# Padding the weight and activation loads to 128 and 112 partitions, with four norm rows and a free instruction order in the key loop

## Chip, cores and metric

The kernel runs on one core of one Trainium2 chip. The metric is the device time of one launch in microseconds (us), lower is better. Every time below is a median of several runs. The engines are PE (matmul; PEld is its weight load), DVE (vector), ACT (scalar), POOL, and SP, which issues most loads and stores here.

## The reference

One transformer block with adaptive layer norm, 2048 tokens, width 576, 32 heads of 18, feed-forward width 4608, all in bf16. Cut to what matters:

```python
mod = (silu(c) @ w_mod).reshape(1, 6, 1, -1)          # shift/scale/gate, twice
sa, ca, ga, sb, cb, gb = (mod[:, i] for i in range(6))
h = layernorm(x) * (1 + ca) + sa
x = x + ga * attention(h)     # q, k, v = h @ wqkv; linear attention: phi = softmax(+-(q or k) @ w_phi)
                              # kv = phi_k^T v ; o = (phi_q kv) / (phi_q sum(phi_k)) ; o @ wo
h = layernorm(x) * (1 + cb) + sb
x = x + gb * (relu(h @ w1) @ w2)
```

## The kernel before

The first layer norm is never applied to x. Instead x, turned (features on partitions, loaded from memory as `xT`), is multiplied by weights that carry the scale, and the mean and the shift come in as extra rows: two unused feature rows, 96 and 97 of the last feature chunk, hold the mean and the standard deviation of each token ("norm rows"), and the weights get matching rows. The 576 features plus padding are cut into NC = 5 chunks of R = 116 partitions. So `xT`, the weights and the modulation weights are all tiles of 116 partitions, and the head groups of the fold (`wq` or `wk` times `w_phi`) are tiles of GR = 108.

```python
R = 116
F = NC * R
X0 = 96
NX = X0 + 2                       # two norm rows, partitions 96 and 97
GR = 108
...
    ctx.enter_context(tc.manual_schedule())        # every engine follows the source order
...
    def load_xT(b):
        t0, nt = BLK[b]
        o = XOFF[t0][0]
        sp.dma_start(xT[0:R, o:o + NC * nt * P], a["xT"][:, o:o + NC * nt * P])

    load(act, ccol[0:R, :], "cc")
    load(act, flat(bdw[0:GR]), "bdw")
    load_x(0, 2)                                   # x itself: 128 partitions, for the statistics
    load(sp, flat(wsc[0:R]), "wsc")                # scale modulation weights
    load(act, ident[:], "ident")
    load(sp, flat(wkT[0:GR]), "wkT")               # key weights, turned
    load_xT(0)
    load(sp, flat(wsh[0:R]), "wsh")                # shift modulation weights
    load_x(2, 2)
    load(sp, flat(wv_raw[0:R]), "wv")
    load_xT(1)
    load_x(4, 2)
    ...                                            # wqT, xT(2), wcb, wsb
    load_x(6, 4)
    load_x(10, 6)
    ...
```

The start computes the scale modulation (`mods([wsc])`), folds the key weights (`fold_k`, five chunks: PE, then ACT, then DVE on one bank pair), the shift modulation, the norm rows of the weights (`rows_mm`, `rows_e`), and the keys of tiles 0 and 1. Then the key loop:

```python
    for t in range(2, NT):
        proj(S0, t - 2, wv)              # values of tile t-2: "the first value projection" is t = 2
        k_sums(t - 1)
        v_e(t - 2, S0)
        k_r(t - 1)
        if t % 2 and t + 1 < NT:
            x_rows(t + 1)                # stat_mm(t+1, 4): statistics transposed into PSUM bank 4
        ...
        proj(S1, t, wk)                  # keys of tile t
        exps(t, S1, E_sb[:, t % NE, :])
        ...
        if t <= 6:
            fold_mm(wqT, t - 2, S2)      # bank pair 4, 5
            fold_e(S2, wq, t - 2, act)
        ...
        if t + 4 < NT:
            bn(0, t + 4)                 # DVE: statistics of tile t+4, needs x of that tile
            if t % 2:
                stats(t + 3)
```

After it come the last queries and the output projection (the tail), then the feed-forward: two matmul loops, `l1` and `l2`, over eight pairs of tiles.

The softmax here doesn't subtract the row's maximum and nothing guards it: scores larger than these inputs give would overflow.

## Time and profile before

| | before |
|---|---|
| time, median of 4 runs (467.32 to 468.48) | 468.12 us |
| span of the profiled run | 466.6 us |
| scale weights' first matmul | 12.9 us |
| first value projection | 40.5 us |
| x tiles 6 to 9 landed | 64 us |
| first feed-forward matmul | 151.4 us |
| feed-forward to the end | 315.1 us |

The first fence holds three lines of the page's overview of before, the span in 40 slices of 11.7 us: the granted PE clock in tenths, the mean busy share of the DMA engines in tenths, and the rate in GB/s.

```profile
PEclk9559559998999999999999999999999999999999
DMA  5346343247370652022123113102211210110000
GB/s 156 114 142 162 114 155 109 98 153 306 75 257 0 243 66 43 14 55 39 41 41 41 43 25 70 41 14 55 41 28 43 50 42 15 30 36 20 0 1 27
```

In the first six slices, 70 us, the clock falls to a half and the loads reach only 114 to 162 GB/s, while the tenth slice shows that 306 is to be had. The next fence is the chain of work that ended last, of before, in its first 66 us: start, duration, and what the time went to.

```profile
2.32 23.87 DMA R<-in_wsh_dram
26.21 5.26 SPq L163
31.52 3.48 SPq L163
35.04 29.12 DMA x_sb<-in_xk_dram
64.19 0.83 DVE st L207 x2
```

The chain is two transfers and the issue of transfers (`SPq`): the shift weights, then the x tiles 6 to 9. Nothing computed is on it until 64.19 us. The waits of before in 0 to 70 us (waiter, releaser, us in total, how often, the longest):

```profile
DVE st L207 <- DMA x_sb<-in_xk_dram: 20.6, 2, 18.5
ACT rk L293 <- DVE Rk L276: 20.2, 2, 18.6
PE PS L237 <- ACT R L511: 16.8, 1, 16.8
PEld L230 <- DMA R<-in_wsc_dram: 6.1, 1, 6.1
```

DVE waited 18.5 us for x; ACT (18.6) waited for DVE's sum behind it, and PE (16.8, the fold of the query weights, L237) for ACT. One wait, seen three times. Last, sums by stretch of before: start and end, length, busy time of PE, PEld, DVE, ACT and POOL, then granted clock, DMA share and GB/s.

```profile
28.00:40.00 12.00, 8.20 (x55) 6.72 (x55) 6.00 (x18) 4.00 (x11) 0.40 (x1) 0.61 0.25 101
50.00:56.00 6.00, 0.68 (x3) 0.36 (x2) 0.00 (x0) 0.00 (x0) 0.00 (x0) 0.50 0.25 106
101.00:112.00 11.00, 9.28 (x69) 6.74 (x68) 6.00 (x12) 6.75 (x13) 5.86 (x8) 0.84 0.90 387
151.60:466.60 315.00, 311.04 (x2873) 254.75 (x2870) 155.70 (x307) 51.59 (x103) 17.03 (x24) 1.00 0.20 43
```

With 116-partition loads in flight the share is 0.25 and the rate 101 to 106 GB/s; with a 128-partition load it is 0.90 and 387. Counted from the packet times of the trace, 4 packets were under way at once for 93% of 50 to 56 us, and 16 for 93% of 101 to 112 us. The feed-forward keeps PE busy for 311 of 315 us and is untouched by the change.

### The profile page before, as it was taken

How to read it: one execution, taken by the hardware profiler on the slowest of the kernel's cores; microseconds unless marked ns; L12 is line 12 of the kernel's file. 1: busy time of each engine (PE TensorE's matmuls, PEld its weight loads, DVE VectorE, ACT ScalarE, POOL GpSimd, SP SyncE). 2: the span in 40 equal slices, each digit the busy share in tenths (PEclk: the TensorE clock that was granted, in tenths of full speed). 3: DMA queues.
4: the chain of work that ended last, by engine and by line, in shares of the span. 5: the costliest groups of instructions: out<-in, count | busy, mean ns of one | idle time of the engine just before them, and what ended most of it. 6: DMA issues, size and time to landing. Idle time of an engine off the chain costs nothing.

```text
span 466.6 us, 8766 instructions
## 1 busy us (share of the span) xinstructions
PE 418.4 (90%) x3810; PEld 336.6 (72%) x3810; DVE 231.5 (50%) x448; ACT 128.8 (28%) x281; POOL 58.6 (13%) x97
## 2 busy tenths in 40 slices
PE   5748229889997999999999999999999999999996
PEld 1536117767875887888888788788888878878885
DVE  2244047755964454475366445537635653453321
ACT  1215128766856320121031013012103101300210
POOL 1002014344930010020011002002001100000000
PEclk9559559998999999999999999999999999999999
DMA  5346343247370652022123113102211210110000
GB/s 156 114 142 162 114 155 109 98 153 306 75 257 0 243 66 43 14 55 39 41 41 41 43 25 70 41 14 55 41 28 43 50 42 15 30 36 20 0 1 27
DMA packets 43752, 35.03 MB, mean 75 GB/s; under 512 B 38541, under 2 KB 40826, under 8 KB 43330
## 3 DMA queue, kind: packets, MB, share of 16 engines
q1 hardware_dynamic: 42754, 23.68, 20.8%
q10 hardware_dynamic: 960, 10.79, 5.9%
q8 instruction: 30, 0.49, 0.4%
q14 instruction: 8, 0.07, 0.0%
HBM read 22.80 MB, written 2.36 MB: 54 GB/s over the span
## 4 chain that ended last, share of the span: by engine, by line
PE 78%; DMA 11%; ACT 5%; SPq 2%; DVE 2%; issue 1%; ACTq 0%
PE PS L663 30%; PE PS L621 28%; PE PS L266 9%; DMA x_sb<-in_xk_dram 6%; DMA R<-in_wsh_dram 5%; PE PS L407 4%; PE PS L628 4%; SPq L163 2%; ACT EQ L271 2%; PE PS L382 1%; ACT E_sb L271 1%; PE PS L325 1%; PE PS L360 1%; DVE Rk L276 1%; ACT RH L244 0%
## 5 line engine op out<-in xcount | busy, mean ns | idle before, releaser
L663 PE MATMUL PS<-R,RH 128*128 128x288 bf16 x1152 | 144.7, 286 | 0.0
L621 PE MATMUL PS<-h,R 128*128 128x256 bf16 x1152 | 134.4, 274 | 0.0
L663 PEld LDWEIGHTS <-RH 128*128 128x128 bf16 x1152 | 112.7, 98 | 28.2
L621 PEld LDWEIGHTS <-R 128*128 128x128 bf16 x1152 | 110.4, 98 | 18.0 <-issue 5.1
L636 ACT ACTIVATE RH<-PS 128x512 bf16<-128x512 f32 x72 | 43.0, 598 | 183.4 <-PE PS L628 162.3
L638 DVE TENSOR_SCALAR RH<-PS 128x512 bf16<-128x512 f32 x72 | 49.8, 692 | 67.9 <-PE PS L628 36.4
L266 PE MATMUL PS<-RH,R 116*128 116x288 bf16 x480 | 70.8, 302 | 5.7 <-ACT EQ L271 3.6
L266 PEld LDWEIGHTS <-R 116*128 116x128 bf16 x480 | 47.8, 103 | 19.8 <-issue 6.9
L666 DVE TENSOR_TENSOR yt<-PS,gb_row 128x288 f32<-128x288 f32 x32 | 14.7, 458 | 63.8 <-PE PS L663 62.7
L207 DVE BATCH_NORM_STATS2 st<-x_sb 128x6 f32<-128x288 bf16 x60 | 24.3, 446 | 21.1 <-DMA x_sb<-in_xk_dram 20.6
L339 POOL TENSOR_TENSOR ratq<-Rq,rq 128x32 f32<-128x32 f32 x16 | 4.1, 254 | 216.5 <-DVE rq L336 216.1
L276 DVE TENSOR_REDUCE Rk<-E_sb 128x64 f32<-128x1152 bf16 x16 | 21.4, 1335 | 14.4 <-ACT E_sb L271 14.4
L271 ACT ACTIVATE E_sb<-PS,rs 128x576 bf16<-128x576 f32 x32 | 22.0, 738 | 6.0 <-PE PS L266 5.8
L271 ACT ACTIVATE EQ<-PS,rs 128x576 bf16<-128x576 f32 x32 | 21.9, 743 | 4.3 <-PE PS L266 4.3
L407 PE MATMUL PS<-wo_sb,oT 128*128 128x288 bf16 x160 | 22.5, 286 | 0.0
L237 PE MATMUL PS<-bdw,R 108*116 108x108 bf16 (+1 forms) x60 | 6.2, 262 | 17.8 <-ACT R L511 16.8
L276 DVE TENSOR_REDUCE Rq<-EQ 128x64 f32<-128x1152 bf16 x16 | 21.5, 1341 | 0.0
L411 ACT ACTIVATE lnv<-mv,eps_t 128x1 f32<-128x1 f32 x16 | 4.7, 296 | 58.8 <-DVE mv L208 57.9
L237 PEld LDWEIGHTS <-R 108*116 108x116 bf16 (+1 forms) x60 | 6.2, 185 | 18.9 <-issue 18.6
L628 PE MATMUL PS<-h,R 64*128 64x256 bf16 x288 | 19.9, 271 | 0.0
L283 POOL TENSOR_TENSOR E_sb<-E_sb,rat 128x576 bf16<-128x576 bf16 x16 | 18.6, 1166 | 1.3
L283 POOL TENSOR_TENSOR EQ<-EQ,ratq 128x576 bf16<-128x576 bf16 x16 | 18.6, 1165 | 1.3
(87 smaller groups left out, 281.1 us busy)
## 6 DMA issues: line engine op xcount, KB each, us to landing
R<-in_w1a_dram ACTq DMA_DIRECT2D x1, 4608.0 KB
R<-in_w2a_dram ACTq DMA_DIRECT2D x1, 2592.0 KB
R<-in_w2b_dram ACTq DMA_DIRECT2D x1, 2592.0 KB
out_dram<-x_sb SPq DMA_DIRECT2D x16, 144.0 KB
R<-in_xT_dram SPq DMA_DIRECT2D x3, 580.0 KB
x_sb<-in_xk_dram SPq DMA_DIRECT2D x3, 288.0 KB
x_sb<-in_xk_dram SPq DMA_DIRECT2D x1, 864.0 KB
R<-in_wkT_dram SPq DMA_DIRECT2D x1, 734.1 KB
```

What stands on the lines that cost most here:

```text
L207: dve.bn_stats(out=s[:, hf, :], in_=x_sb[:, t, hf * HD:(hf + 1) * HD])
L266: pe.matmul(pr[:, k, 0:HD], lhsT=xt(t, ck), rhs=w[0:R, ck, k * HD:(k + 1) * HD], start=(ck == 0), stop=(ck == NC - 1))
L271: act.activation(out=E.rearrange("p (b h s e) -> p b h s e", b=2, s=2, e=DH)[:, :, :, s, :], in_=pr[:, :, 0:HD].rearrange("p b (h e) -> p ...
L276: dve.tensor_reduce(out=Rr, in_=E.rearrange("p (c e) -> p c e", e=DH), axis=AXX, op=ALU.add)
L283: eng.tensor_tensor(out=e, in0=e, in1=ratio.unsqueeze(2).to_broadcast([P, H, DH]), op=ALU.mult)
L407: pe.matmul(pr[:, k, 0:HD], lhsT=oT[:, t % 2, ci, :], rhs=wo_sb[:, ci, k * HD:(k + 1) * HD], start=(ci == 0 and not add_x), stop=(ci == NC ...
L621: pe.matmul(PS[:, 2 * u + hf, n * 256:n * 256 + 256], lhsT=w1a[:, ci, jj * P:(jj + 1) * P], rhs=hb[:, ci, :], start=(n == 0 and ci == 0), ...
L628: pe.matmul(PS[:, 2 * u + hf, n * 256:n * 256 + 256], lhsT=w1b[b0:b0 + 64, j * P:(j + 1) * P], rhs=hb[b0:b0 + 64, 4, :], start=False, stop ...
L636: act.activation(out=o, in_=i, func=ACT.Relu)
L638: dve.tensor_relu(o, i)
L663: pe.matmul(PS[:, bank, 0:HD], lhsT=H1[:, j % 18, j // 18, tt * P:(tt + 1) * P], rhs=w2[j // 18][:, j % 18, k * HD:(k + 1) * HD], start=(j ...
L666: dve.tensor_tensor(out=yt[:, k, :], in0=PS[:, bank, 0:HD], in1=gb_row[:, c], op=ALU.mult)
```

## The change

The intent: send every large load as 128 (or 112) full partitions, to have it at a rate like the 387 GB/s of the 128-partition load in before instead of the 101 to 106 of the 116-partition ones; put the weights that the start needs first ahead of x; carry the mean as two bf16 parts, with a second pair of norm rows, for accuracy; and let the instruction scheduler order the key loop and the tail, where before the source order was kept on every engine. In the start only PE keeps the source order. The diff, cut to its core:

```diff
-NX = X0 + 2
+NX = X0 + 4
 GR = 108
+GP = 112
@@
-    ctx.enter_context(tc.manual_schedule())
+    PEO = {mybir.EngineType.PE}
@@ loads (all 116-row ones alike; the arrays in memory are padded with zero rows)
-        sp.dma_start(xT[0:R, o:o + NC * nt * P], a["xT"][:, o:o + NC * nt * P])
+        sp.dma_start(xT[:, o:o + NC * nt * P], a["xT"][:, o:o + NC * nt * P])
-    load(act, ccol[0:R, :], "cc")
-    load(act, flat(bdw[0:GR]), "bdw")
+    load(act, ccol[:], "cc")
+    load(act, flat(bdw[0:GP]), "bdw")
+    load(act, ident[:], "ident")
+    load(sp, flat(wsc), "wsc")
+    load(sp, flat(wkT[0:GP]), "wkT")
+    load_xT(0)
     load_x(0, 2)
-    load(sp, flat(wsc[0:R]), "wsc")
-    load(act, ident[:], "ident")
-    load(sp, flat(wkT[0:GR]), "wkT")
-    load_xT(0)
-    load(sp, flat(wsh[0:R]), "wsh")
+    load(sp, flat(wsh), "wsh")
+    load(sp, flat(wv_raw), "wv")
     load_x(2, 2)
-    load(sp, flat(wv_raw[0:R]), "wv")
... (the rest in the old order, padded)
@@ norm rows: mean as two parts
-        act.activation(out=sc[:, t % 4:t % 4 + n, X0], in_=mv[:, 0, t:t + n, 0], func=ACT.Copy)
+        act.activation(out=sc[:, t % 4:t % 4 + n, X0:X0 + 3:2], in_=mv[:, 0, t:t + n, 0:1].to_broadcast([P, n, 2]), func=ACT.Copy)
+        pool.tensor_tensor(out=sc[:, t % 4:t % 4 + n, X0 + 3], in0=mv[:, 0, t:t + n, 0], in1=sc[:, t % 4:t % 4 + n, X0], op=ALU.subtract)
@@ rows_e: one copy becomes two steps
+        act.activation(out=h, in_=i, func=ACT.Copy)
+        dve.scalar_tensor_tensor(out=o, in0=h, scalar=mk[X0:NX, :], in1=i, op0=ALU.mult, op1=ALU.add)
@@ order
-    spin(14, 0)
+    order = ExitStack()
+    order.enter_context(tc.manual_schedule(engines=PEO))
+    spin(11, 0)
... (the start rewritten: folds first, statistics of x after them)
+    kv_eps()
+    order.close()                       # from here on free, until the feed-forward
... (key loop and tail as they were)
+    ctx.enter_context(tc.manual_schedule())
     NB = NT // 2
```

More of the change, by code (lines that the diff above doesn't have):

```diff
@@ L87, in tile_block @@
     wo_sb = small([P, NC, D], BF16, "wo_sb")
-    ident = small([P, P], BF16, "ident")
+    ident = small([P, P + 1], BF16, "ident")
+    mk = small([P, 1], FP32, "mk")
     mask = small([P, KVW], BF16, "mask")
@@ L121, in tile_block @@
     yt = small([P, 2, HD], FP32, "yt")
+    tmpr = yt.rearrange("p a b -> p (a b)").bitcast(BF16)[:, 0:D]
     stg = yt.rearrange("p a b -> p (a b)").bitcast(BF16)[:, 0:4 * P]
@@ L180, in tile_block @@
     load(sp, epsr[:], "epsr")
-    load(sp, flat(wqT[0:GR]), "wqT")
+    load(sp, flat(wqT[0:GP]), "wqT")
     load_xT(2)
-    load(sp, flat(wcb[0:R]), "wcb")
-    load(sp, flat(wsb[0:R]), "wsb")
+    load(sp, flat(wcb), "wcb")
+    load(sp, flat(wsb), "wsb")
     load_x(6, 4)
@@ L187, in tile_block @@
     load_xT(3)
-    load(sp, flat(wga[0:R]), "wga")
+    load(sp, flat(wga), "wga")
     load(sp, flat(wo_sb), "wo")
-    load(sp, flat(wgb[0:R]), "wgb")
+    load(sp, flat(wgb), "wgb")
     load_xT(4)
@@ L195, in tile_block @@
     pool.memset(eps_t[:], EPS)
+    pool.tensor_copy(mk[:], ident[:, P:P + 1])
     pool.memset(m98[:], 0.0)
@@ L219, in stat_mm @@
         for j in range(n):
-            pe.transpose(bf(PS[:, bank, :])[0:NX, j * P:(j + 1) * P], sc[:, (t + j) % 4, :], ident[:])
+            pe.transpose(bf(PS[:, bank, :])[0:NX, j * P:(j + 1) * P], sc[:, (t + j) % 4, :], ident[:, 0:P])
         return bf(PS[:, bank, :])[X0:NX, 0:n * P]
@@ L254, in rows_mm, with rows_e @@
                           start=(ck == 0), stop=(ck == NC - 1))
-    def rows_e(pr, dst, eng):
-        o, i = v2(dst[X0:NX, 4, :]), pr[X0:NX, :, 0:HD]
-        if eng is act:
-            act.activation(out=o, in_=i, func=ACT.Copy)
-        else:
-            eng.tensor_copy(out=o, in_=i)
+    def rows_e(pr, dst):
+        o, i, h = v2(dst[X0:NX, 4, :]), pr[X0:NX, :, 0:HD], v2(tmpr[X0:NX, :])
+        act.activation(out=h, in_=i, func=ACT.Copy)
+        dve.scalar_tensor_tensor(out=o, in0=h, scalar=mk[X0:NX, :], in1=i, op0=ALU.mult, op1=ALU.add)
     def proj(pr, t, w, cks=range(NC)):
@@ L395, in o_turn_pe @@
         for ci in range(NC):
-            pe.transpose(pt[:, ci * P:(ci + 1) * P], o_sb[:, t % 2, ci * P:(ci + 1) * P], ident[:])
+            pe.transpose(pt[:, ci * P:(ci + 1) * P], o_sb[:, t % 2, ci * P:(ci + 1) * P], ident[:, 0:P])
         act.activation(out=flat(oT[:, t % 2]), in_=pt[:, 0:640], func=ACT.Copy)
@@ L404, in wo_mm @@
             if add_x:
-                pe.matmul(pr[:, k, 0:HD], lhsT=ident[:], rhs=x_sb[:, t, k * HD:(k + 1) * HD], start=True, stop=False)
+                pe.matmul(pr[:, k, 0:HD], lhsT=ident[:, 0:P], rhs=x_sb[:, t, k * HD:(k + 1) * HD], start=True, stop=False)
             for ci in range(NC):
@@ L437, in h2_pe @@
         for ci in range(NC):
-            pe.transpose(pt[:, ci * P:(ci + 1) * P], xn[:, t % 2, ci * P:(ci + 1) * P], ident[:])
+            pe.transpose(pt[:, ci * P:(ci + 1) * P], xn[:, t % 2, ci * P:(ci + 1) * P], ident[:, 0:P])
         for ci in range(NC):
@@ L453, in tile_block, with fold_k @@
     dve.tensor_tensor(out=siluc[0:R, :], in0=ccol[0:R, :], in1=sg[0:R, 2, :], op=ALU.mult)
+    mods([wsc], None, R, 7, idle=0)
+    dve.tensor_scalar(out=ca1[0:R, :], in0=PS[0:R, 7, 0:NC], scalar1=1.0, scalar2=None, op0=ALU.add)
+    for q in (0, 2, 3):
+        dve.tensor_scalar(out=m98[0:R, :, X0 + q], in0=ca1[0:R, :], scalar1=-1.0, scalar2=None, op0=ALU.mult)
+    def fold_k(ck):
+        pr = pair(2 + ck % 2)
+        fold_mm(wkT, ck, pr)
+        fold_e(pr, wk, ck, dve if ck < 4 else act)
+    spin(2, 1)
+    fold_k(0)
+    fold_k(1)
+    spin(1, 1)
+    fold_k(2)
+    proj(S0, 0, wk, [0])
+    fold_k(3)
+    proj(S0, 0, wk, [1])
+    fold_k(4)
     bn(0, 0)
@@ L456, in tile_block @@
     stats(0)
-    mods([wsc], None, R, 7, idle=0)
-    dve.tensor_scalar(out=ca1[0:R, :], in0=PS[0:R, 7, 0:NC], scalar1=1.0, scalar2=None, op0=ALU.add)
-    dve.tensor_scalar(out=m98[0:R, :, X0], in0=ca1[0:R, :], scalar1=-1.0, scalar2=None, op0=ALU.mult)
-    sr = stat_mm(0, 2)
-    act.activation(out=stg[X0:NX, 0:2 * P], in_=sr, func=ACT.Copy)
-    pool.tensor_copy(xt_rows(0, 2), stg[X0:NX, 0:2 * P])
-    spin(3, 1)
-    def fold_k(ck):
-        pr = pair(2 + ck % 2)
-        fold_mm(wkT, ck, pr)
-        fold_e(pr, wk, ck, dve)
-    fold_k(0)
-    fold_k(1)
-    fold_k(2)
-    proj(S0, 0, wk, [0])
-    fold_k(3)
     mods([wsh], None, R, 2)
     act.activation(out=m98[0:R, :, X0 + 1], in_=PS[0:R, 2, 0:NC], func=ACT.Copy)
-    proj(S0, 0, wk, [1])
-    fold_k(4)
+    sr = stat_mm(0, 3)
+    act.activation(out=xt_rows(0, 2), in_=sr, func=ACT.Copy)
+    proj(S0, 0, wk, [2, 3])
+    rows_mm(wfold, S3)
+    rows_e(S3, wk)
+    for ck in range(NC):
+        dve.tensor_scalar(out=wv[0:R, ck, :], in0=wv_raw[0:R, ck, :], scalar1=ca1[0:R, ck:ck + 1], scalar2=None, op0=ALU.mult)
+    proj(S1, 1, wk, range(4))
+    rows_mm(wv_raw, S2)
+    proj(S0, 0, wk, [4])
+    exps(0, S0, E_sb[:, 0, :])
+    proj(S1, 1, wk, [4])
+    exps(1, S1, E_sb[:, 1, :])
+    rows_e(S2, wv)
     for t in range(2, 4):
@@ L481, in tile_block @@
     stats(2)
-    proj(S0, 0, wk, [2])
-    sr = stat_mm(2, 3)
-    act.activation(out=stg[X0:NX, 2 * P:], in_=sr, func=ACT.Copy)
-    pool.tensor_copy(xt_rows(2, 2), stg[X0:NX, 2 * P:])
-    proj(S0, 0, wk, [3])
-    rows_mm(wfold, S3)
-    rows_e(S3, wk, act)
-    proj(S1, 1, wk, range(4))
-    for ck in range(NC):
-        dve.tensor_scalar(out=wv[0:R, ck, :], in0=wv_raw[0:R, ck, :], scalar1=ca1[0:R, ck:ck + 1], scalar2=None, op0=ALU.mult)
-    proj(S0, 0, wk, [4])
-    exps(0, S0, E_sb[:, 0, :])
-    rows_mm(wv_raw, S2)
-    proj(S1, 1, wk, [4])
-    rows_e(S2, wv, act)
-    exps(1, S1, E_sb[:, 1, :])
+    sr = stat_mm(2, 6)
+    act.activation(out=xt_rows(2, 2), in_=sr, func=ACT.Copy)
+    kv_eps()
+    order.close()
     for t in range(4, 6):
@@ L500, in tile_block @@
     stats(4)
-    kv_eps()
     k_sums(0)
@@ L542, in tile_block @@
             rows_mm(wfold, S2)
-            rows_e(S2, wq, act)
+            rows_e(S2, wq)
         else:
@@ L708, in _rows @@
 def _rows():
-    r = list(range(464 + X0)) + [-1, -1] + list(range(464 + X0, D))
+    r = list(range(464 + X0)) + [-1] * (NX - X0) + list(range(464 + X0, D))
     return r + [-1] * (F - len(r))
@@ L718, in _layout, with pad @@
     on = rows >= 0
+    def pad(m, n):
+        return np.concatenate([m, np.zeros((n - m.shape[0],) + m.shape[1:], dt)], axis=0)
     def feat(m):
@@ L723, in feat @@
         z[on] = m[rows[on]]
-        return z.reshape(NC, R, -1).transpose(1, 0, 2)
+        return pad(z.reshape(NC, R, -1).transpose(1, 0, 2), P)
     def cols(m):
@@ L753, in groups @@
             z[i, :nh * DH] = m[h0 * DH:(h0 + nh) * DH]
-        return flat(z.transpose(1, 0, 2))
+        return flat(pad(z.transpose(1, 0, 2), GP))
     o["wqT"] = groups(np.ascontiguousarray(cols(w[:, 0:D].T.copy())))
@@ L761, in _layout @@
             bd[i, h * DH:(h + 1) * DH, h * DH:(h + 1) * DH] = g["A_w_phi"][h0 + h]
-    o["bdw"] = flat(bd.transpose(1, 0, 2))
-    o["ident"] = np.eye(P).astype(dt)
+    o["bdw"] = flat(pad(bd.transpose(1, 0, 2), GP))
+    idm = np.zeros((P, P + 1), np.float32)
+    idm[:, :P] = np.eye(P)
+    idm[X0 + 2, P] = -1.0
+    o["ident"] = idm.astype(dt)
     mk = np.zeros((P, KVW), np.float32)
```

## The prediction

> **What bounds the kernel now.** The span is 466.6 us. From 151.6 us on it is the feed-forward part, 315 us, with PE busy 311 us at granted clock 1.00 (sums by stretch): nothing of the change touches it. Before it, loads decide. The chain of waits is almost all DMA up to 64 us: shift weights (landed 26.2 us), then x tiles 6 to 9 (64.2 us). Waits: the first norm matmul waited for the scale weights until 12.9 us; DVE's statistics waited 18.5 us for tiles 6 to 9; behind it PE stood 16.8 us, until 67.5 us.
>
> [...]In 28 to 40 and 50 to 56 us, with 116-partition loads in flight, the DMA share is 0.25 and the rate 101 to 106 GB/s; in 101 to 112 us, with 128-partition weights, 0.90 and 387 GB/s. [...]
>
> **What the change does.** Padding adds about 8% of bytes[...]. Scale and key weights go ahead of x. Estimate from the rates above: 8.2 MB up to tiles 6 to 9, at 350 to 390 GB/s from 3 us on, land at 25 to 28 us instead of 64; scale weights at 6.5 us instead of 12.9, shift weights at 12 instead of 26.
>
> Then start-up is bound by its own chain: scale modulation matmuls (2.5 to 4 us), five folds (ACT 0.74, DVE 0.76 us each, about 6 us), row matmuls (1.4), the row copy, now in two steps (0.64 on ACT, about 0.75 on DVE, estimate), last projection and two exponentials (1.38 each). That puts the first value projection at about 22 us; it was at 42.2. Gain: about 20 us, all on the path.
>
> The 17 us stall in the loop's second pass goes away: gain 17 us, plus 1 to 2 because PE ran at granted clock 0.50 after it until 71 us.
>
> Added: two more norm rows (same matmul counts), a tiny subtract on POOL per statistics pair, two-step row copies three times: under 1.5 us on the path.
>
> Free order in the loop: from 67.5 to 151.6 us PE is busy about 73 of 84 us, so some 10 us of gaps at most, and ACT is nearly as full up to the eighth pass. I count 1 us gained, plus or minus 5.
>
> **Predicted:** 468 - 20 - 17 - 2 + 1.5 - 1, about 429 us; range 419 to 439. Faster by over 2%: 0.97; within 2%: 0.02; slower: 0.01.
>
> **What would show it.** The chain of waits up to 60 us no longer DMA but ACT, DVE and PE; over 300 GB/s in the first 25 us; scale modulation at about 7 us; first value projection at 20 to 25 us; no wait of DVE's statistics for x over 2 us; the first feed-forward matmul at about 113 us; the feed-forward still 315 us. If the free order matters, the stretch from first value projection to feed-forward, less the stall, moves from 92 us by more than 3.
>
> **What would make it wrong.** Loads short of 300 GB/s[...] and a shorter stall left over; the start chain at clock 0.5 with PE thinly used, 3 to 5 us more; a free order that puts a late-loaded statistic or a projection ahead of urgent work, 5 to 10 us more; or one that fills the gaps, 5 us less.

468 - 20 - 17 - 2 + 1.5 - 1 comes to 429.5. That the padded loads would reach 350 to 390 GB/s is the estimate from the 387 of the 128-partition weights in before; for 112 partitions nothing had been measured. The 0.75 us of DVE for the row copy is an estimate too, like the 0.75 to 0.76 us that DVE took in before for other steps over 576 columns (L305, L248); in after the step took 0.82 us (L265). From 67.5 to 110 us of before PE was busy 38.0 of 42.5 us and ACT 30.6. A clock of 0.50 with PE thinly used, one of the risks named, stood in before from 50 to 56 us, with PE busy 0.68 us of 6.

## The result, and the profile after

The time is 424.75 us (median of 4 runs, 424.45 to 425.0) against 468.12 us. The ratio is 0.9076, 95% interval 0.906 to 0.9091. Ratios here are the mean time of one kernel's fast runs over that of the other's of the same rounds, so not quite the ratio of the medians quoted.

| | before | after |
|---|---|---|
| time | 468.12 us | 424.75 us |
| span of the profiled run | 466.6 | 423.0 |
| scale weights' first matmul | 12.9 | 6.9 |
| first value projection | 40.5 | 25.5 |
| x tiles 6 to 9, last packet | 63.7 | 26.6 |
| first feed-forward matmul | 151.4 | 108.6 |
| from first value projection to there | 110.9 | 83.2 |
| feed-forward to the end | 315.1 | 314.4 |

The span lost 43.6 us: 15.1 in the start, 27.7 between the first value projection and the feed-forward, 0.7 in the feed-forward. The overview lines of after (40 slices of 10.6 us):

```profile
PEclk9699999999999999999999999999999999999999
DMA  8994298700642114101210321041113200120000
GB/s 261 373 419 179 57 409 224 179 2 2 245 66 46 31 31 73 31 29 39 51 46 16 60 45 29 16 78 27 31 29 73 47 15 18 19 43 15 2 5 25
```

The second and third slices carry 373 and 419 GB/s, and only one slice has a low clock. In the chain of after, some pieces of the first 30 us:

```profile
0.76 5.24 DMA ccol<-in_cc_dram
10.68 1.42 DVE R L253 x2
14.03 1.67 PE PS L235 x25
18.10 2.40 PE PS L258 x10
20.50 1.59 PE PS L270 x8
24.02 2.64 ACT E_sb L275 x4
```

Only one load is left on it, the vector c (`ccol`, 1.25 KB); the rest is folds, modulation, norm rows, exponentials. Among the forty longest waits of after in its first 70 us, the longest for a load is that of ACT for c; the next is 2.2 us, of POOL for `ident`, and none is for x:

```profile
ACT sg L456 <- DMA ccol<-in_cc_dram: 4.0, 1, 4.0
```

Sums by stretch of after, from the first packets to the landing of x tiles 6 to 9, and the feed-forward:

```profile
3.00:26.60 23.60, 18.49 (x156) 13.96 (x155) 13.10 (x37) 10.09 (x25) 1.42 (x4) 0.86 1.03 373
108.60:423.00 314.40, 310.44 (x2874) 254.35 (x2871) 156.11 (x309) 51.90 (x104) 17.02 (x24) 1.00 0.19 43
```

A DMA share over 1 is no slip: packets are counted by their own times, and in this stretch up to 22 packets were under way at once on the 16 engines.

### The profile page after: what moved, and what is told of

Same layout as the page of the kernel before. It is cut to its first block, busy times and chain, and to the rows that moved or that the text cites. A ratio compares the mean times of both kernels' runs of the same rounds, so it can differ in the third digit from the quotient of the medians.

```text
span 423.0 us, 8791 instructions
## 1 busy us (share of the span) xinstructions
PE 407.5 (96%) x3807; PEld 329.7 (78%) x3807; DVE 229.3 (54%) x452; ACT 126.6 (30%) x282; POOL 57.6 (14%) x104
## 4 chain that ended last, share of the span: by engine, by line
PE 85%; ACT 8%; DVE 4%; DMA 1%; issue 1%; POOL 0%; ACTq 0%
PE PS L669 33%; PE PS L627 30%; PE PS L270 8%; PE PS L634 4%; PE PS L411 4%; ACT E_sb L275 2%; ACT EQ L275 2%; PE PS L386 1%; DMA ccol<-in_cc_dram 1%; PE PS L235 1%; DVE Rk L280 1%; PE PS L258 1%; ACT RH L249 1%; PE PS L329 1%; DVE R L253 1%
## 5 line engine op out<-in xcount | busy, mean ns | idle before, releaser
L270 PE MATMUL PS<-RH,R 116*128 116x288 bf16 x480 | 66.0, 289 | 3.1 <-ACT E_sb L275 1.3
L270 PEld LDWEIGHTS <-R 116*128 116x128 bf16 x480 | 46.5, 99 | 17.0 <-issue 5.5
L411 PEld LDWEIGHTS <-oT 128*128 128x128 bf16 x160 | 15.6, 98 | 4.1 <-ACT oT L401 0.2
L701 DVE TENSOR_TENSOR x_sb<-x_sb,PS 128x576 bf16<-128x576 bf16 x14 | 10.6, 754 | 13.9 <-PE PS L411 13.9
## 6 DMA issues: line engine op xcount, KB each, us to landing
R<-in_wcb_dram SPq DMA_DIRECT2D x1, 800.0 KB, 11.6
```

The costliest lines, as they stand in the source:

```text
L270: pe.matmul(pr[:, k, 0:HD], lhsT=xt(t, ck), rhs=w[0:R, ck, k * HD:(k + 1) * HD], start=(ck == 0), stop=(ck == NC - 1))
L411: pe.matmul(pr[:, k, 0:HD], lhsT=oT[:, t % 2, ci, :], rhs=wo_sb[:, ci, k * HD:(k + 1) * HD], start=(ci == 0 and not add_x), stop=(ci == NC ...
```

## The experiments

Twelve kernels ran; all gave correct results. The theory (A): the share of the DMA engines that the loads keep busy (in before 0.25 with 116 partitions, 0.90 with 128) set the time, and nearly all of the gain is the padding; the free order is worth about 1 us. Rival B: the free order takes away the stall. Rival C: weights first and the rewritten start shorten the start. What came out is a fourth thing: the free order pays, but only once the loads are padded.

### 1. Padding alone

The kernel before with the padded loads; the list of instructions on every engine is otherwise that of before.

```diff
-        sp.dma_start(xT[0:R, o:o ...
+        sp.dma_start(xT[:, o:o ...
-    load(sp, flat(wsc[0:R]), "wsc")
+    load(sp, flat(wsc), "wsc")
... (all others alike, arrays padded)
```

> The kernel before with the padded, 128- and 112-partition loads and nothing else; the order of instructions on every engine is that of before. Theory A[...]: loads run at over 300 GB/s, x tiles 6 to 9 land at about 28 us instead of 64, the 16.8 us stall of PE goes, first value projection at about 26 us instead of 42.2; time 433 us (428 to 440). Theory B (the free order takes away the stall, loads matter little): over 450 us. Theory C (weights ahead of x and the reordered start are what shortens the start): stall goes, start stays near 38 to 42 us, about 447 us.

Measured: 435.59 us (435.2 to 436.47), ratio 0.9311 (0.929 to 0.9332). The loads of the start ran at 379 GB/s:

```profile
3.00:26.00 23.00, 16.93 (x138) 12.22 (x137) 11.30 (x33) 7.51 (x21) 0.80 (x2) 0.78 1.03 379
```

The first value projection came at 27.2 us, the feed-forward at 119.0, 91.8 us later. So the padding alone takes 32.5 us of the 43.4, in both places: 13.3 us in the start and 19.1 in the loop (110.9 to 91.8), which is the stall of 16.8 us and 2.3 us more; before ran at half clock from the end of the stall to 71.4 us, which may be most of those 2.3, but no run separates them. B and C do not explain this run.

### 2. Free order alone

```diff
-    ctx.enter_context(tc.manual_schedule())
+    order = ExitStack()
+    order.enter_context(tc.manual_schedule())
@@ after the keys of tiles 0 and 1
+    order.close()
@@ before the feed-forward
+    ctx.enter_context(tc.manual_schedule())
```

> The kernel before with free order from the first loop pass to the feed-forward, and nothing else[...]. Theory A: the projections of later passes need data that has not landed, so the stall stays at 10 us or more; 460 to 468 us. Theory B: DVE no longer waits in order for x tiles 6 to 9 and PE is fed meanwhile; 450 us or less.

Measured: 466.84 us (466.2 to 467.78), ratio 0.9983 (0.9958 to 1.0008): the same as before. The waits of this kernel in 38 to 80 us:

```profile
PE PS L267 <- DVE v_sb L306: 15.9, 2, 14.5
DVE st L208 <- DMA x_sb<-in_xk_dram: 14.5, 1, 14.5
```

DVE still waits 14.5 us for the same x and PE 14.5 us for DVE. Later comes a wait that before does not have:

```profile
PE PS L361 <- ACT R L513: 7.7, 1, 7.7
ACT R L513 <- DMA R<-in_xT_dram: 7.5, 1, 7.5
```

ACT waited for the last block of `xT`, whose last packet came at 106.7 us, against 92.8 in before. With the free order ACT issued the first feed-forward weights (4608 KB) at 81.9 us instead of 99.5, and most of that block moved only when they were through; that this delayed it is argued from the trace, no run separates it. So the wait for x became 4 us shorter, and a wait for another load took its place. B falls.

### 3. The rest of the change with the old widths

The kernel after with 116- and 108-partition loads; the order of the instructions on every engine is that of after.

```diff
-GP = 112
+GP = 108
+PW = 116          # feature loads: tile[0:PW], arrays padded to PW
```

> The kernel after with the loads back at 116 and 108 partitions; the order of instructions on every engine is that of after. Theory A: DMA share 0.25 and about 105 GB/s while such loads run, x tiles 6 to 9 land at about 60 us, most of the gain is gone: 455 us (450 to 463). Theory C: weights first and free order keep a good part: 440 us or less.

Measured: 469.9 us (469.34 to 471.04), ratio 1.0045 (1.0021 to 1.0069). I had expected 455. The wait of ACT for c alone was 10.5 us here, against 4.0 in after; that the narrow scale weights, issued at the same moment, made c late was not shown. And ACT waited 10.6 us for the last block of `xT`, as in experiment 2. Nothing of the gain is left: first value projection at 41.8 us, x tiles 6 to 9 by 65.5 us, 111.2 us from there to the feed-forward. C falls. Sums of this kernel in a stretch with only 116-partition loads:

```profile
50.00:56.00 6.00, 4.80 (x55) 3.89 (x55) 1.35 (x1) 5.84 (x13) 3.07 (x6) 1.00 0.26 105
```

### 4 and 5. Other widths: 124 and 120

Same kernel with `PW = 124` and `PW = 120` (and 112 for the head groups). Again the order of instructions is that of after.

> The kernel after with 124-partition loads (112 stays): 8 partitions more than 116, 4 more than 120, same order on every engine. [...]DMA share 0.25 and 105 GB/s again and the time is back at that of 116 or over it: 470 us (464 to 476), although 120 gave 428. If the count of partitions mattered smoothly, it would lie between 424.75 and 428.

Measured: 476.65 us (474.5 to 479.38), ratio 1.0192 (1.0148 to 1.0236). That is just above the expected range; four partitions fewer than in after cost 52 us. A stretch of this kernel:

```profile
13.00:18.00 5.00, 1.72 (x13) 1.49 (x14) 0.52 (x3) 0.21 (x1) 0.72 (x1) 0.50 0.26 98
```

The share is a quarter again, 0.26.

> The kernel after with 120 instead of 128 partitions in the loads that were 116 (112 stays): 4 partitions more than 116, same order on every engine. Theory A[...] DMA share 0.5 and 200 to 215 GB/s while such loads run, x tiles 6 to 9 land at about 36 us; 431 us (428 to 438). If only the amount of padding or rows near 128 counted, it would be like width 116 (over 450) or like after (425).

Measured: 428.06 us (426.94 to 429.17), ratio 0.9148 (0.912 to 0.9175). The time hit the expectation, but for no good reason: the share of 0.5 and the 200 to 215 GB/s are twice those of 116, and the number of engines on which that doubling rested, no run shows. Two stretches of this kernel, in which 120-partition loads made up about 80% (13 to 18 us) and two thirds (21 to 30 us) of the bytes, counted by packet size:

```profile
13.00:18.00 5.00, 4.90 (x44) 4.41 (x42) 3.35 (x9) 2.76 (x4) 0.00 (x0) 0.50 0.99 217
```

```profile
21.00:30.00 9.00, 7.93 (x55) 6.04 (x54) 6.63 (x14) 5.84 (x19) 0.40 (x2) 0.85 1.02 244
```

Of the packets of these loads 15 were under way at once for 62% of the time from 13 to 18 us (with 116, in 50 to 56 us of before, 4 for 93%), and the share is 0.99 to 1.02, not the 0.5 I expected; a 5,760 B packet took 391 ns in the median, against 220 ns in after. At the pace of after, 15 packets at once would give some 350 GB/s (an estimate: 15/16 of the 373 GB/s of after, where 16 were under way for 66% of the time from 3 to 26.6 us and more for nearly all of the rest); 217 to 244 came, which is near the 200 to 215 that I had expected. So nearly as many packets were under way as with 128 partitions, each of them slower. But the trace does not name a packet's engine, so how many engines 120 used, and why it is slower than 128, stays open. What these three widths do show is that the time is not smooth in the width: 116 and 124 are slow (469.9 and 476.65 us), 120 and 128 are not (428.06 and 424.75). That is what theory A needs.

### 6. The source order in the loop of after

```diff
     order.close()
+    order.enter_context(tc.manual_schedule())
@@ before the feed-forward
+    order.close()
     ctx.enter_context(tc.manual_schedule())
```

> The kernel after with the free order taken from the loop only: from the first loop pass to the feed-forward all engines follow the source order again; loads and start as in after. From the first value projection to the feed-forward after took 83.2 us and the padded kernel in before's order 91.8 us. Theory A2 (free order is worth this once the loads are fast): the stretch is 91 to 92 us, time 433 us (431 to 435), start as in after. Rival D (the loop gained from the start: higher granted clock, statistics and weights done earlier): stretch 83 to 86 us, time 425 to 428 us.

Measured: 434.44 us (433.14 to 437.33), ratio 0.9298 (0.9254 to 0.9341). The start is that of after (first value projection 25.6 us); the feed-forward begins at 115.3, 89.7 us later, and then takes 317.4 us instead of 314.4; 2.1 us of that is a wait at its beginning, for the last query exponentials. So the free order in the loop is worth 9.7 us once the loads are fast. The rival D falls.

### 7. Padding and free order, nothing else

Experiments 1 and 2 together: old load order, old start, two norm rows.

> The kernel before with padded loads and free order in the loop; load order, start and two norm rows as in before. A2: start like the padded kernel alone (first value projection 27 us), loop stretch like after (83 to 84 us), 427 us (425 to 429). D: loop stretch stays near 92 us, 435 us.

Measured: 424.87 us (424.37 to 426.99), ratio 0.9091 (0.9065 to 0.9117): the same as after. This closes the account:

| time, us | source order in the loop | free order in the loop |
|---|---|---|
| 116 and 108 partitions | 468.12 | 466.84 |
| 128 and 112 partitions | 435.59 | 424.87 |

The order of the loads, the rewritten start and the two further norm rows together add nothing that shows. The free order is worth 1.3 us (within the noise) on the slow loads and 10.7 us on the fast ones: on the slow ones PE still stood 14.5 us behind the wait for x and another 7.7 us behind the last block of `xT` (experiment 2).

### 8. Two norm rows in after

```diff
-NX = X0 + 4
+NX = X0 + 2
... (one-step rows_e on ACT; no subtract; one column of m98)
```

> The kernel after with two norm rows instead of four (one-step row copy on ACT, no subtract on POOL). The two-step copies of the start sit behind PE work that is as long, and statistics have slack: I expect 0.5 to 1 us less, 424 us (423 to 425). A rival that the four rows cost what the start lost against the prediction (5 us) expects 420 us.

Measured: 424.22 us (422.66 to 426.15), ratio 0.907 (0.904 to 0.9101). The interval covers after's 0.9076: four rows cost nothing that this run can show, and surely not 5 us.

### 9. One suspected wait of the source order taken away

Where does the free order gain? In the loop in source order the largest wait of PE that after hasn't got was at the transposes of the statistics (L225), which write bank 4, a bank that ACT still empties from the fold. The edit, in the loop of experiment 6:

```diff
-        sr = stat_mm(t, 4)
+        sr = stat_mm(t, 0)
@@ in the loop
-        if t % 2 and t + 1 < NT:
-            x_rows(t + 1)
         ...
         exps(t, S1, E_sb[:, t % NE, :])
+        if t % 2 and t + 1 < NT:
+            x_rows(t + 1)
```

> The loop in source order again, with one change to it: in the odd passes the transposes of the statistics come after the key projection and write bank 0, which is free by then, instead of bank 4, where PE waited for ACT to empty the weight fold. In the trace of the loop in source order PE waited 2.5 us at these transposes for ACT's fold copy, 1.3 us for ACT's query exponentials, and 1.8 us more for ACT's row copy before the gate rows and a projection. If the free order gains chiefly by moving these transposes out of the way: those waits go, 429 to 431 us against 434.4. If it gains by many small moves of all kinds: 432 to 434 us.

Measured: 433.93 us (430.29 to 436.36), ratio 0.9256 (0.9217 to 0.9295), against 434.44 and 0.9298 (0.9254 to 0.9341): no difference shown. Its six executions follow the mean granted clock (430.3 and 430.9 us at 0.992, 436.4 at 0.973); at 0.984 one took 433.5 us, against 434.4 and 434.5 in experiment 6, so a gain of about 1 us is not excluded. PE's waits in the source-order loop (25 to 119 us) before the edit, experiment 6:

```profile
PE PS L225 <- ACT R L251: 2.5, 2, 1.3
PE PS L628 <- ACT EQ L275: 2.1, 1, 2.1
PE PS L225 <- ACT EQ L275: 1.3, 3, 0.8
```

and with it, experiment 9:

```profile
PE PS L628 <- ACT EQ L275: 2.1, 1, 2.1
PE PS L270 <- ACT R L518: 2.0, 4, 1.0
PE PS L225 <- DVE v_sb L309: 2.0, 4, 0.6
```

The waits on ACT at L225 went, and as much came back at L225 for DVE and at the projections (L270) for ACT's row copy. So the gain of the free order does not sit in this one wait. When the key exponentials of tiles 2, 3, 8, 13 and 15 ended shows it piling up in small steps: at 32.1, 36.8, 58.5, 85.6 and 94.0 us in source order (experiment 6), at 30.9, 33.9, 54.3, 81.3 and 88.1 us in after, from starts 0.2 us apart. Differences of 1.2, 2.9, 4.2, 4.3 and 5.9 us, and about 3 us more where the tail meets the feed-forward.

A part of this goes with the clock. The sums of 25.5 to 45 us, first of experiment 6, then of after:

```profile
25.50:45.00 19.50, 16.25 (x140) 12.13 (x140) 14.96 (x27) 15.47 (x41) 9.12 (x17) 0.91 0.57 232
25.50:45.00 19.50, 17.68 (x173) 13.76 (x173) 17.03 (x34) 17.52 (x51) 8.85 (x21) 1.00 0.57 231
```

In experiment 6 the clock was 0.50 from 31.1 to 34.5 and again from 116.4 to 119.9 us, with PE busy all the time; in after it stayed at 1.00 from 21.6 us on. Half of these 6.8 us, up to 3.4 of the 9.7, is an estimate of what that cost, as matmuls at 0.50 took about twice as long (2.61 against 1.39 us in experiment 10). All three padded kernels with the source order in the loop (experiments 1, 6, 9) show two such stretches after the start, and none of the seven with the free order and fast loads does (after, experiments 5, 7, 8, 10, 11, 12). Some 7 us remain without the clock, an estimate from single executions: at the same mean clock of 0.984 experiment 6 took 434.4 and 434.5 us and experiment 7 took 427.0. Whether the source order brings the slow stretches was not tested.

### 10. Keeping PE busy in the start

The start of after came 3.5 us later than predicted. In it the granted clock was 0.50 from 14.8 to 21.6 us. The edit fills PE's gaps with idle matmuls:

```diff
-    spin(1, 1)
+    spin(4, 1)
     fold_k(2)
@@
     proj(S0, 0, wk, [1])
+    spin(3, 3)
     fold_k(4)
@@
+    spin(4, 3)
     sr = stat_mm(0, 3)
```

> The kernel after with ten more idle matmuls at the three places of the start where PE stood (before folds 2 and 4 and before the first statistics transposes), so that PE stays busy and the granted clock stays at 1.00 where it fell to 0.50 from 14.8 to 21.6 us. If the halved clock costs the start what its stretched matmuls suggest (shift modulation 1.8 us against 0.8, row matmuls 2.6 against 1.4, eight projections 1.8 against 1.1): first value projection at 23 us instead of 25.5, 422 us (421 to 423.5). If the clock does not follow or PE is not what the start waits for: 424.5 to 425.5 us.

Measured: 422.41 us (422.19 to 422.45), ratio 0.9023 (0.9009 to 0.9037): 2.3 us faster than after. The same stretch, first of after, then of this kernel; the clock is the third number from the end:

```profile
14.80:21.60 6.80, 5.80 (x33) 4.61 (x32) 3.57 (x13) 2.40 (x10) 0.31 (x1) 0.50 1.04 356
```

```profile
14.80:21.60 6.80, 6.16 (x51) 4.83 (x51) 5.60 (x19) 3.64 (x15) 0.59 (x2) 1.00 1.03 354
```

The norm-row matmuls in the timelines (start, duration, count), first of after:

```profile
17.89 2.61 PE L258 MATMUL PS<-R,m 116*100 116x288 bf16 x10
```

and of this kernel:

```profile
16.89 1.39 PE L258 MATMUL PS<-R,m 116*100 116x288 bf16 x10
```

They take 1.39 us instead of 2.61, and the first value projection comes at 23.1 us instead of 25.5: the 2.4 us of the start is the whole gain (83.2 us from there to the feed-forward in both). The four runs agree within 0.3 us (after: 0.6).

What makes the clock fall is not shown. In after no wait of PE in the start was over 1.3 us, and the clock still fell to 0.50 at 14.8 us. PE was busy 2.6 us of the last 3.4 before the fall, but only 2.2 and 2.4 us of the two stretches of 3.4 before, which the clock survived. The half-clock stretches in the start were 3.4, 6.8 and 10.2 us long in three kernels (experiments 8, after, 11). These three scattered by 0.6 to 3.5 us from run to run, the two whose profiled run had none (experiments 10 and 12) by 0.3 and 0.9 us.

### 11 and 12. The load of c first, alone and with the idle matmuls

```diff
-    load(act, ccol[:], "cc")
+    load(sp, ccol[:], "cc")          # first on SP's queue
```

> The kernel after with the 1.25 KB load of c issued first on SP's queue, ahead of the scale weights, instead of on ACT's. In after, c landed at 6.0 us, later than the scale weights, and PE waited 1.25 us for what is computed from it. Expected: c lands by 4.5 us, scale weights about 0.4 us later than in after, first norm matmul at 6.1 instead of 6.9 us, time 424.0 us (423.5 to 424.5). If c is late because of its place beside large transfers and not of the queue, nothing moves: 424.75 us.

Measured: 425.11 us (423.87 to 426.07), ratio 0.908 (0.9061 to 0.9099): nothing shown. The first norm matmul did come earlier, at 6.4 instead of 6.9 us, but this trace had 10.2 us of half clock in the start instead of 6.8, which could hide half a microsecond. Hence the last run, with both edits:

> The kernel after with both small edits: the ten more idle matmuls and the load of c first on SP's queue. Alone the load of c moved nothing (425.11 us), but in its trace the clock was at 0.50 for 10.3 us of the start (13.2 to 23.5) against 6.8 us in after, which may have hidden a gain: its first norm matmul came 0.5 us earlier. If that is so, with the clock held by the idle matmuls the gain shows: 421.9 us (421.6 to 422.2) against 422.41. If the start does not wait for c in a way that counts: 422.4 us.

Measured: 422.51 us (422.26 to 423.13), ratio 0.9019 (0.9005 to 0.9033), against 422.41: no gain. In the trace the first scale matmul came at 6.0 instead of 6.8 us, but the first value projection only 0.2 us earlier (22.9 against 23.1): the folds then wait for the key weights (PEld 0.78 us, until 9.0 us) and for ACT and DVE (PE 0.44 us for DVE). How late c lands differs with what is issued beside it: 5.2 us from issue to landing in after, with the scale weights issued at the same moment, and 3.2 us in experiment 1, where a load of x was; whether the neighbour is the cause was not tested. The idle matmuls alone are the version that beats both kernels; the load of c first need not be kept.

## Why the prediction was right, and where it was not

The time, 424.75 us, lies within the range 419 to 439; what the prediction said of the times of the loads was right, and the sum came out well partly by luck, because two terms were off in opposite directions: the start by 4.9 us, the free order by about 9.

- **Narrow loads bound the first 64 us: right, and shown.** Padding alone took 32.5 us; 116 and 124 partitions are slow, 128 fast, with the same instructions in the same order. With 116 alone under way (50 to 56 us of before) there were 4 packets at once for 93% of the time, in the start of after 16 or more for over 97%; a 5,760 B packet took 220 ns in the median in both kernels, so the narrow loads had fewer packets under way, not slower ones. The shares of 0.25 to 0.26 at 98 to 106 GB/s for 116 and 124 are a quarter of the engines' time; the point at 120 does not fit in rate (experiment 5). The rule from which the prediction took its numbers of engines was not shown.
- **Landing times: right.** Last packet of tiles 6 to 9 at 26.6 us (said 25 to 28), of the shift weights at 11.6 us (said 12), rate 373 GB/s (said 350 to 390), with loads of 0.3 to 0.9 MB.
- **The stall of 17 us and 1 to 2 us of slow clock after it: right in sum.** 110.9 to 91.8 us in experiment 1, so 19.1; that the part beyond the stall is the clock is argued, not shown.
- **"That puts the first value projection at about 22 us; it was at 42.2. Gain: about 20 us": too large.** It came at 25.5 us. The 42.2 us was a misreading: the ten matmuls at 42.23 us are the key projection of the first pass; the value projection stands before them at 40.53. So the start gained 15.1 us. Of the 3.5 us that 22 fell short, 2.4 are the half clock (experiment 10 gets 23.1); c, which landed at 6.0 us, is worth 0.2 of it (experiment 12 against 10). The half clock stood in the prediction as a risk of "3 to 5 us more", but not in the sum. The shift modulation (1.8 us in after) was not in the sum either.
- **"Free order in the loop ... I count 1 us gained, plus or minus 5": the mis-sized term.** It is worth 9.7 to 10.7 us on fast loads. The prediction knew of some 10 us of PE gaps at most and took ACT, "nearly as full", to keep them. PE's busy time in this part fell by little, 79.4 us of 91.8 in experiment 1 against 78.0 of 83.1 in after, so it is gaps that went: from about 12 us to about 5. Up to 3.4 us of the gain may be the two half-clock stretches of the source order, an estimate (experiment 9).
- **The two further norm rows: cost under what can be shown** (said under 1.5 us).
- **Feed-forward: 314.4 us, as predicted.**

In which single waits the free order gains, and whether it is the order that keeps the clock up, is not settled: experiment 9 removed the largest wait and it came back elsewhere.

## What to carry to other kernels

Look at the partition count of every load, not only at its bytes: here 116 and 124 partitions gave a share of 0.25 to 0.26 at 98 to 106 GB/s, and zero rows up to 128 gave 373. Where a stretch with one load alone shows such a share, try a few zero rows and measure, for the width in between, 120, gave 217 to 244. Measure a scheduling change together with the load change that it has to live with: a better order was worth nothing behind late loads, where it also brought a large load forward, to all appearance into the way of a narrow one (experiment 2), and 10 us once the loads were in time. When the start has many short dependent steps, read the granted clock there; ten idle matmuls bought 2.3 us. Compare the clocks of two kernels before putting a difference down to their order.
